# Two chunk groups into K, oT in two halves, V copied on ACT ahead of the exponentials, and a later selection in a recurrent attention kernel

## Chip, cores and metric

One core of a Trainium2 chip. The metric is device microseconds of one execution of the whole program; lower is better. Most executions of one kernel agree within 0.3%. Some versions scatter more.

PE is the matmul engine (PEld its weight loads), DVE the vector engine, ACT the scalar engine, POOL the engine that here mainly issues DMAs, SP the queue of the other DMAs.

## The reference, cut to what matters

Part A is attention with a recurrent memory: 2048 tokens in 64 segments of 32, 32 heads of 128, width 640. Eight memory rows are carried from segment to segment.

```python
mem = mem0                                   # 8 rows of 640
for s in range(64):
    h = concat([mem, x[32*s : 32*s+32]])     # 40 rows
    q, k, v = h @ Wq, h @ Wk, h @ Wv         # 640 -> 32 heads of 128
    p = softmax(mask(q @ k.T * scale))
    o = (p @ v) @ Wo                         # back to 640
    mem = o[:8]                              # the next segment needs these
    outs.append(o[8:])
```

Part B is a gated feed-forward net over all rows. It runs after the loop, and the change does not touch it.

## The kernel before

The loop is one pass per segment, fully unrolled. A helper records every operation with the keys (tiles) it reads and writes, and a solver turns keys into semaphore waits. This rule of the solver:

```python
for k in op.w:                               # keys that the operation writes
    bank = k[0] == "B"
    if k in writer:                          # it waits for the last writer of the same key
        deps[writer[k]] = deps.get(writer[k], False) or not bank
    for o in readers.get(k, ()):             # and for the readers since
        deps.setdefault(o, False)
```

The parts of a pass that the change touches, in the order in which the kernel before records them (`...` marks cuts):

```python
# K and Q projections, from the memory rows (act_r) of the pass before
project(a, ks, 1, (0, 1), BQ, spare=40)            # K, five chunks of 128
to_tok(BQ[0], 0, "act"); to_tok(BQ[1], 1, "dve")
...
project(a, ks, 0, (0, 1), (P0, P1), spare=40)      # Q
to_tok(P0, 2, "act"); to_tok(P1, 3, "dve")
...
project(a, ks, 2, (0, 1), (P2, P3), (0, 1), spare=16)       # V, chunks 0 and 1
pick_mem(T0)                                       # "selection": the memory rows of Q, 8 matmuls
copy_op("dve", Qr[:, :, q, 0:M], ..., [B(T0)], [("Qm", q)])
evac_k(KS, ("KS",), t0, nr, M, "dve")
project(a, ks, 2, (0, 1), (P2, P3), (2, 3, 4), spare=24)    # V, chunks 2 to 4
to_v(P3, Vp, 1, ("Vp",), "dve")                    # V's upper half to SBUF
scores(s)
exp_mem()                                          # ACT writes om, DVE makes Pbd from it
to_v(P2, Vp, 0, ("Vp",), "act")                    # V's lower half to SBUF
exp_x()                                            # ACT writes Px
...
filler(0); filler(1)                               # PE work of other segments, to fill waits
pv_mem(s)                                          # "memory PV": needs Pbd and Vp
...
norm_om(); filler(2); filler(3)
trans_om(...)                                      # PE transposes om, DVE copies it to oT
filler(4)
wo_pass(T1, ...)                                   # Wo: 128 small matmuls
to_act(s + 1, B(T1), bank(T1)[:, 0:160])           # memory rows, transposed, for the next K
pv_x(s, P0)                                        # PE work while DVE does to_act
```

`to_act` is one DVE transpose into TBf and one DVE cast into act_r. `spare` is room for padding: the kernel pads PE's instruction stream so that each Wo pass stands at a chosen place within a line of 256 instructions (`MARKS`). Both V copies write the same key, `("Vp",)`.

The tiles in the profile lines: `ps` is the accumulators that PE writes, `tok` the projections K and Q as copied out of them, Vp the V of this pass and Vr that of the other rows. `om` and `Px` are the exponentials of the scores (om of those against the memory rows; it later holds their result), and `Pbd` is om masked into the form that the memory PV multiplies with V.

The softmax here doesn't subtract the row's maximum and nothing guards it: scores larger than these inputs give would overflow.

## Time and profile before

The kernel before took 1122.48 us at first (median of 3) and 1121.92 us over four runs.

| of the kernel before | us or share | where it is read |
|---|---|---|
| span of the profiled run | 1118.8 | the page |
| PE busy | 95% | the page, part 1 |
| PE in the chain that ended last | 87% | the page, part 4 |
| one pass (2 to 61, mean) | 13.60 | starts of PE's groups in the timeline |

The page's first line of part 1 and the two of part 4:

```profile
PE 1063.8 (95%) x28016; PEld 505.4 (45%) x23471; DVE 593.1 (53%) x1477; ACT 353.7 (32%) x729; POOL 286.5 (26%) x575
...
PE 87%; DMA 5%; DVE 3%; SPq 3%; issue 1%; POOL 0%; ACT 0%; DVEq 0%; ACTq 0%
PE ps L419 25%; PE ps L397 24%; PE ps L636 13%; PE ps L1010 10%; PE ps L1043 3%; PE ps L564 3%; PE ps L650 3%; SPq L357 3%; DMA Wo<-in_A_Wo_dram 3%; PE ps L601 2%; DVE TBf L548 2%; PE ps L448 2%; DMA Wu<-in_B_W_up_dram 1%; DVE act_r L549 1%; PE ps L616 1%
```

PE is the bottleneck and hardly ever idle. DVE is in the chain only with TBf and act_r, the hand-over of the memory rows from Wo to the next K. ACT is not in it (0%). So the question is what happens in the few tenths of a microsecond per pass in which PE has nothing to do.

The timeline around the exponentials of pass 35. The columns are start, duration, engine, line, operation, tiles, and in brackets the idle time before it with what ended it. Scores started at S = 536.25:

```profile
536.46 0.69 DVE L461 CAST Vp<-ps 128x512 bf16<-128x512 f32 x1 [0.48 <-PE ps L397]
537.16 0.28 ACT L574 ACTIVATE om<-ps 128x128 bf16<-128x128 f32 x1 [2.67 <-PE ps L564]
537.33 0.59 ACT L459 ACTIVATE Vp<-ps 128x512 bf16<-128x512 f32 x1
537.47 0.49 DVE L577 TENSOR_TENSOR Pbd<-om,mbd 128x256 bf16<-128x256 bf16 x2 [0.32 <-ACT om L574]
537.82 0.30 PE L601 MATMUL ps<-Vr,Pbd 128*32 128x129 bf16 x8
538.07 0.30 PE L601 MATMUL ps<-Vp,Pbd 128*32 128x129 bf16 x8
```

The order om (ACT), Pbd (DVE), memory PV (PE) is a chain. PE starts the memory PV at S+1.57 here, and its filler reaches nearly up to that. ACT's V copy comes after om and holds nobody up.

From the waits of the same kernel (who waited for whom: us in total, times, longest):

```profile
PEld ps L448 <- DVE tok L461: 38.9, 61, 0.6
PEld ps L601 <- DVE Pbd L577: 33.8, 63, 0.9
ACT Vp L459 <- DVE Vp L461: 2.3, 1, 2.3
```

The last line is easily passed over: only 2.3 us. But it says that ACT's copy of V waits for DVE's. In all but one pass ACT has om to do first, so the wait does not show.

The groups of the DVE operations that the change cuts in two (count | busy, mean ns of one | idle before):

```profile
L548 DVE STREAM_TRANSPOSE TBf<-ps 128x160 f32<-128x160 f32 x64 | 22.4, 349 | 93.1 <-PE ps L636 93.0
L461 DVE COPY oT<-ps 128x256 bf16<-128x256 bf16 x63 | 18.4, 292 | 27.9 <-PE ps L616 27.9
L549 DVE CAST act_r<-TBf 128x40 bf16<-128x40 f32 x64 | 11.7, 183 | 2.2
```

And PE around selection (L448) in pass 35:

```profile
534.32 0.39 PE L397 MATMUL ps<-W,act_r 128*32 128x512 bf16 x4
534.65 0.37 PE L448 MATMUL ps<-ident,tok 128*128 128x32 bf16 x8
```

From the last group of V to selection it is 0.33 us here, where one group of four to the next takes 0.215 us. About 0.1 us is lost.

### The profile page before, as it was taken

The page shows a single profiled execution, that of the slowest core. Times are in us where ns is not written, and L with a number is a line of the kernel's source. Part 1 is how long each engine was busy: PE and PEld are TensorE (multiplying, and loading weights), DVE is VectorE, ACT ScalarE, POOL GpSimd, SP SyncE. Part 2 cuts the span into 40 slices and gives each one's busy share as a digit, 9 for nine tenths or more (in the row PEclk, how much of TensorE's full clock was granted, in tenths as well). Part 3 has the DMA queues.
Part 4 walks back from the last instruction along what each step waited for, and adds up shares of the span by engine and source line. Part 5 has one row for each costly group of instructions (what it writes and reads, how often), then busy time and mean ns, then how long its engine had stood idle before and what let it go on. Part 6 is the DMA issues. An engine that isn't in the chain of part 4 may idle for free.

```text
span 1118.8 us, 55562 instructions
## 1 busy us (share of the span) xinstructions
PE 1063.8 (95%) x28016; PEld 505.4 (45%) x23471; DVE 593.1 (53%) x1477; ACT 353.7 (32%) x729; POOL 286.5 (26%) x575
## 2 busy tenths in 40 slices
PE   5679999999999999999999999999999969999998
PEld 3344544444445454444444444444444435343443
DVE  3235555555556565666666666565656533463422
ACT  2113333333333333333433333333333312131220
POOL 1013333333333232323232414142423321000000
PEclk9879999999999999999999999999999998999999
DMA  9936454545363546465655566555544476122100
GB/s 353 381 80 109 88 110 88 108 87 108 79 111 79 111 79 107 82 122 101 117 106 114 111 115 111 100 97 93 95 89 92 91 219 173 47 77 77 24 18 24
DMA packets 290824, 122.40 MB, mean 109 GB/s; under 512 B 267008, under 2 KB 280224, under 8 KB 290592
## 3 DMA queue, kind: packets, MB, share of 16 engines
q1 hardware_dynamic: 271216, 94.95, 40.1%
q0 software_dynamic: 19184, 23.89, 9.2%
q8 instruction: 202, 3.31, 1.2%
q14 instruction: 30, 0.25, 0.1%
q10 hardware_dynamic: 192, 0.01, 0.0%
HBM read 36.79 MB, written 7.21 MB: 39 GB/s over the span
## 4 chain that ended last, share of the span: by engine, by line
PE 87%; DMA 5%; DVE 3%; SPq 3%; issue 1%; POOL 0%; ACT 0%; DVEq 0%; ACTq 0%
PE ps L419 25%; PE ps L397 24%; PE ps L636 13%; PE ps L1010 10%; PE ps L1043 3%; PE ps L564 3%; PE ps L650 3%; SPq L357 3%; DMA Wo<-in_A_Wo_dram 3%; PE ps L601 2%; DVE TBf L548 2%; PE ps L448 2%; DMA Wu<-in_B_W_up_dram 1%; DVE act_r L549 1%; PE ps L616 1%
## 5 line engine op out<-in xcount | busy, mean ns | idle before, releaser
L419 PE MATMUL ps<-W,act_r 128*32 128x512 bf16 x4277 | 398.5, 388 | 13.2 <-DMA W<-in_A_Wq_dram 3.4
L397 PE MATMUL ps<-W,act_r 128*32 128x512 bf16 x3603 | 352.8, 379 | 0.3 <-issue 0.3
L357 POOL DMA_DIRECT2D Vr<-Vp x376 | 187.5, 506 | 469.9 <-ACT Vp L459 296.1
L419 PEld LDWEIGHTS ps<-W,act_r 128*32 128x32 bf16 x4277 | 116.6, 98 | 274.6 <-issue 220.3
L459 ACT ACTIVATE tok<-ps 128x512 bf16<-128x512 f32 x191 | 110.4, 594 | 256.7 <-PE ps L397 230.1
L461 DVE CAST tok<-ps 128x512 bf16<-128x512 f32 x131 | 90.5, 691 | 148.7 <-PE ps L397 125.3
L636 PE MATMUL ps<-Wo,oT 128*32 128x160 bf16 x8320 | 160.0, 235 | 9.7 <-DMA Wo<-in_A_Wo_dram 7.4
L636 PEld LDWEIGHTS ps<-Wo,oT 128*32 128x32 bf16 x8320 | 145.3, 98 | 35.9 <-DVE oT L461 25.9
L419 PE MATMUL ps<-W,act_e 128*32 128x512 bf16 x900 | 90.9, 381 | 0.0
L397 PE MATMUL ps<-W,act_e 128*32 128x512 bf16 x900 | 90.4, 379 | 0.0
L689 DVE TENSOR_TENSOR ox<-ps,rx 128x512 bf16<-128x512 f32 x128 | 82.4, 685 | 2.2
L459 ACT ACTIVATE Qr<-QS 128x512 bf16<-128x512 bf16 (+3 forms) x107 | 70.0, 682 | 33.8 <-DMA QS<-tok 33.4
L357 POOL DMA_DIRECT2D attn_d<-wtok x64 | 46.6, 728 | 123.4 <-ACT wtok L459 123.3
L548 DVE STREAM_TRANSPOSE TBf<-ps 128x160 f32<-128x160 f32 x64 | 22.4, 349 | 93.1 <-PE ps L636 93.0
L1010 PE MATMUL ps<-xn2T,Wu 128*128 128x512 bf16 x260 | 65.7, 384 | 5.7 <-DMA Wu<-in_B_W_up_dram 5.7
L1025 DVE TENSOR_TENSOR hT<-g,ps 128x512 bf16<-128x512 bf16 (+1 forms) x56 | 38.5, 687 | 61.3 <-PE ps L1010 57.5
L1010 PE MATMUL ps<-xn2T,Wg 128*128 128x512 bf16 x246 | 62.3, 383 | 5.6 <-issue 5.3
L574 ACT ACTIVATE om<-ps 128x128 bf16<-128x128 f32 x63 | 17.5, 277 | 145.6 <-PE ps L564 142.9
L1043 PE MATMUL ps<-Wd,hT 128*128 128x320 bf16 (+1 forms) x240 | 63.3, 300 | 0.0
L1023 ACT ACTIVATE g<-ps 128x512 bf16<-128x512 f32 (+1 forms) x56 | 32.5, 592 | 95.6 <-PE ps L1010 95.6
L461 DVE CAST Vp<-ps 128x512 bf16<-128x512 f32 x64 | 44.3, 692 | 29.1 <-PE ps L397 25.1
L397 PE MATMUL ps<-Wd,hT 128*128 128x320 bf16 x208 | 56.9, 299 | 0.0
(104 smaller groups left out, 1146.4 us busy)
## 6 DMA issues: line engine op xcount, KB each, us to landing
Vr<-Vp POOLq DMA_DIRECT2D x124, 48.8 KB, 1.9
W<-in_A_Wk_dram SPq DMA_DIRECT2D x2, 2560.0 KB, 13.2
W<-in_A_Wq_dram SPq DMA_DIRECT2D x2, 2560.0 KB, 25.5
W<-in_A_Wv_dram SPq DMA_DIRECT2D x2, 2560.0 KB, 27.7
Wo<-in_A_Wo_dram SPq DMA_DIRECT2D x2, 2560.0 KB, 28.3
xt<-in_A_x_dram SPq DMA_DIRECT2D x30, 160.0 KB, 3.6
Vr<-Vp POOLq DMA_DIRECT2D x128, 32.5 KB, 1.9
attn_d<-wtok POOLq DMA_DIRECT2D x64, 40.0 KB, 2.8
```

The source lines that it names most:

```text
L357: add(eng, lambda e: e.dma_start(dst, src), r=r, w=w, dma=True)
L397: return pe.add_instruction(mybir.InstMatmult(name=nc.get_next_instruction_name(), engine=mybir.EngineType.PE, ins=[pe.lower_ap(rhs), pe.l ...
L419: ins = pe.matmul(*a, start=(c == 0), stop=(c == DC - 1), skip_group_check=True)
L459: add("act", lambda a: a.activation(dst, src, ACTF.Copy), r=r, w=w)
L461: add("dve", lambda v: v.tensor_copy(dst, src), r=r, w=w)
L548: add("dve", lambda v: v.transpose(TBf[:].rearrange("p c t -> p (c t)"), src), r=[wkey], w=[("TBf",)])
L564: i = pe.matmul(bank((P0, P1)[g % 2])[p:p + (M if a else 32), 40 * k:40 * k + 40], lh, Qr[:, h, q, :], start=True, stop=True, skip_group_c ...
L636: i = pe.matmul(bank(bk)[32 * gg:32 * gg + 32, 0:160], oT[:, hb, :], w[:, gg], start=(hb == ORDER[0]), stop=(hb == ORDER[31]), skip_group_ ...
L689: add("dve", lambda v, kh=kh: v.tensor_tensor(ox[:, :, kh, :], src[:, :, kh, 0:128], ap(rx, kh, [[2, 4], [0, 128]]), ALU.mult), r=[B(b0 + ...
L1010: ins = pe.matmul(bank(bk), w[:, c, lo:lo + 128], xn2T[par][:, c, :], start=(c == 0), stop=(c == DC - 1))
L1025: add("dve", lambda v: v.tensor_tensor(hT[par][lo:128, j, :], g1[gi][lo:128, :], bank(bu)[lo:128, :], ALU.mult), r=[B(bu), ("g1", gi)], w= ...
L1043: i = pe.matmul(*a, start=(j == 0), stop=(j == FC - 1), skip_group_check=True)
```

## The change

Its intent is to take PE's short waits away:

1. the memory rows enter act_r in two groups, chunks 0 and 1 first, so that K can start on the first group;
2. selection stands one V chunk later, so that the copy of Q that it reads is surely done;
3. oT is transposed into two banks and copied in two halves, so that the first half of Wo needs only the first copy;
4. ACT copies V before its exponentials, so that V is ready early.

```diff
     def to_act(s, wkey, src):
         b, j = s // 4, s % 4
-        add("dve", lambda v: v.transpose(TBf[:].rearrange("p c t -> p (c t)"), src), r=[wkey], w=[("TBf",)])
-        add("dve", lambda v: v.tensor_copy(act_r[b % 2][:, j, :, 0:M], TBf[:, :, 0:M]), r=[("TBf",)],
-            w=[("act", b % 2, j, "m")])
+        for n, (lo, hi) in enumerate(((0, 2), (2, DC))):
+            add("dve", lambda v, lo=lo, hi=hi: v.transpose(TBf[:, lo:hi, :].rearrange("p c t -> p (c t)"),
+                                                           src[:, 32 * lo:32 * hi]), r=[wkey], w=[("TBf", n)])
+            add("dve", lambda v, lo=lo, hi=hi: v.tensor_copy(act_r[b % 2][:, j, lo:hi, 0:M], TBf[:, lo:hi, 0:M]),
+                r=[("TBf", n)], w=[("act", b % 2, j, "mn"[n])])
 ...
     def trans_om(tile):
-        (both transposes into bank T1, one DVE copy of 256 columns, key ("oT", "m"))
+        for a, b in enumerate((T0, P3)):
+            (transpose a into bank b)
+        for a, b in enumerate((T0, P3)):
+            (DVE copy of 128 columns from bank b, key ("oT", "mn"[a]))
 ...
     # Wo, half hf
-            op = add("pe", f, r=[("oT", "m"), ("oT", "x"), ("Wo", hf)], w=[B(bk)])
+            op = add("pe", f, r=[("oT", "mn"[hf]), ("oT", "x"), ("Wo", hf)], w=[B(bk)])
 ...
-            project(a, ks, 1, (0, 1), BQ, spare=40)
+            project(a, ks, 1, (0, 1), BQ, (0, 1), spare=16)
+            ks = ks + kn
+            project(a, ks, 1, (0, 1), BQ, (2, 3, 4), spare=24)
 ...
-            project(a, ks, 2, (0, 1), (P2, P3), (0, 1), spare=16)
+            project(a, ks, 2, (0, 1), (P2, P3), (0, 1, 2), spare=24)
             (selection)
-            project(a, ks, 2, (0, 1), (P2, P3), (2, 3, 4), spare=24)
+            project(a, ks, 2, (0, 1), (P2, P3), (3, 4), spare=16)
             to_v(P3, Vp, 1, ("Vp",), "dve")
 ...
+            to_v(P2, Vp, 0, ("Vp",), "act")
             scores(s)
             exp_mem()
-            to_v(P2, Vp, 0, ("Vp",), "act")
             exp_x()
```

The lines in round brackets are cuts. The rest of the diff gives the new keys to the places that read or write them.

More of the change, by code (lines that the diff above doesn't have):

```diff
@@ L341, in build_kernel @@
         add("dve", lambda v, b=b: v.memset(bank(b), 0.0), w=[B(b)])
-    add("dve", lambda v: v.memset(oT[:], 0.0), w=[("oT", "m"), ("oT", "x")])
+    add("dve", lambda v: v.memset(oT[:], 0.0), w=[("oT", "m"), ("oT", "n"), ("oT", "x")])
     add("pool", lambda p: p.memset(ap(Vp, Dh, [[VW, 8], [1, VW - Dh]]), 1.0), w=[("Vp1",)])
@@ L345, in build_kernel @@
         add("pool", lambda p, i=i: p.memset(act_r[i][:], 0.0),
-            w=[("act", i, j, "m") for j in range(4)] + [("act", i, "x")])
+            w=[("act", i, j, h) for j in range(4) for h in "mn"] + [("act", i, "x")])
     for i in range(RING // SEG):
@@ L523, in ln1_back @@
             for e in range(2):
-                copy(act_r[1][:, e, :, :], src[:, :, 32 * e:32 * e + 32], [("act", 1, e, "m"), ("act", 1, "x")])
+                copy(act_r[1][:, e, :, :], src[:, :, 32 * e:32 * e + 32], [("act", 1, e, "m"), ("act", 1, e, "n"), ("act", 1, "x")])
             return
@@ L538, in pass_act @@
         b, j = s // 4, s % 4
-        return act_r[b % 2][:, j], [("act", b % 2, j, "m"), ("act", b % 2, "x", j), ("act", b % 2, "x")]
+        return act_r[b % 2][:, j], [("act", b % 2, j, "m"), ("act", b % 2, "x", j), ("act", b % 2, "x")], \
+            [("act", b % 2, j, "n")]
     def rider_tokens(s):
@@ L612, in trans_om, with f @@
     def trans_om(tile):
-        def f(pe):
-            for a in range(2):
+        for a, b in enumerate((T0, P3)):
+            def f(pe, a=a, b=b):
                 for c in range(0, 128, tile):
-                    i = pe.matmul(bank_bf(T1)[c:c + tile, a * 128:(a + 1) * 128], om[:, a, c:c + tile],
-                                  ident[:, :], is_transpose=True)
-            return i
-        add("pe", f, r=[("om",), ("ident",)], w=[B(T1)])
-        copy_op("dve", ap(oT, 0, [[2 * SEG, 8], [16 * SEG, 2], [SEG, 2], [1, M]]),
-                bank_bf(T1)[:, 0:256].rearrange("p (k g e q) -> p k g e q", k=8, g=2, e=2), [B(T1)], [("oT", "m")])
+                    i = pe.matmul(bank_bf(b)[c:c + tile, 0:128], om[:, a, c:c + tile], ident[:, :], is_transpose=True)
+                return i
+            add("pe", f, r=[("om",), ("ident",)], w=[B(b)])
+        for a, b in enumerate((T0, P3)):
+            copy_op("dve", ap(oT, 8 * SEG * a, [[2 * SEG, 4], [16 * SEG, 2], [SEG, 2], [1, M]]),
+                    bank_bf(b)[:, 0:128].rearrange("p (k g e q) -> p k g e q", k=4, g=2, e=2), [B(b)], [("oT", "mn"[a])])
     def head_of(n):
@@ L694, in trans_ox @@
         dma_t(oT[:].rearrange("p h t -> p (h t)").rearrange("p (k r) -> p k r", r=128),
-              ox[:].rearrange("p k g d -> p (k g d)"), [("ox", 0), ("ox", 1)], [("oT", "m"), ("oT", "x")])
+              ox[:].rearrange("p k g d -> p (k g d)"), [("ox", 0), ("ox", 1)], [("oT", "m"), ("oT", "n"), ("oT", "x")])
     def copy_oTe(s):
         o = M * (s % 4)
-        copy_op("dve", oTe[:, :, o:o + M], oT[:, :, 0:M], [("oT", "m")], [("oTe", s % 4)])
+        copy_op("dve", oTe[:, :, o:o + M], oT[:, :, 0:M], [("oT", "m"), ("oT", "n")], [("oTe", s % 4)])
     def attn_keys(i):
@@ L763, in build_kernel @@
     to_act(0, ("w0",), w0)
-    a0, k0 = pass_act(0)
-    groups = [(a0, k0)] + [(act_r[1][:, e], [("act", 1, e, "m"), ("act", 1, "x")]) for e in range(2)]
+    a0, k0, k1 = pass_act(0)
+    groups = [(a0, k0 + k1)] + [(act_r[1][:, e], [("act", 1, e, "m"), ("act", 1, e, "n"), ("act", 1, "x")]) for e in range(2)]
     gbanks = (BQ, (T0, T1), (P0, P1))
@@ L895, in build_kernel @@
         if s > 0:
-            a, ks = pass_act(s)
+            a, ks, kn = pass_act(s)
             t0, nr = rider_tokens(s)
-            project(a, ks, 1, (0, 1), BQ, spare=40)
+            project(a, ks, 1, (0, 1), BQ, (0, 1), spare=16)
+            ks = ks + kn
+            project(a, ks, 1, (0, 1), BQ, (2, 3, 4), spare=24)
             to_tok(BQ[0], 0, "act")
@@ L951, in build_kernel @@
         if s % 4 == 1 and s >= 5:
-            copy_op("dve", oTn[:, :, :], oT[:, :, 0:M], [("oT", "m")], [("oTn",)])
+            copy_op("dve", oTn[:, :, :], oT[:, :, 0:M], [("oT", "m"), ("oT", "n")], [("oTn",)])
         elif s > 0:
```

## The prediction

> **What bounds the kernel.** The page's busy table has PE at 95% of the 1118.8 us span; the chain that ended last is 87% PE. Between about 79 and 895 us run 60 alike recurrent passes of 13.6 us (timeline). The change can only win or lose in a pass's short PE stalls, read from a group's last matmul to the next group's first, starts both, less the usual step (four 512-column matmuls per 0.215 us):
> - Wo to the next K projection: DVE transpose TBf 0.35 us, then the act_r cast 0.18 us, in the chain in every pass (3% together). PE waits about 0.25 us.
> - Before selection: 0.31 instead of 0.21 us, waiting for DVE's tok copy.
> - Before Wo, in the two passes of four with 32-wide transposes: 0.345 instead of 0.206 us, behind DVE's oT copy (0.29 us).
> - Before the memory PV: only 0.03 to 0.07 us. Chain: scores start (S), ACT's om exponential at S+0.77 to 0.93, Pbd, PV at S+1.43 to 1.57.
>
> **What the change does to each.**
> 1. Two chunk groups. A DVE op here costs about 0.14 to 0.18 us plus its elements (fitted to the 160- and 40-element durations), so an estimated 0.25 + 0.155 us for the first group instead of 0.35 + 0.18: K restarts 0.14 us earlier. The second group is ready about 0.45 us after that and needed after 0.86 us: hidden. 60 passes: -8.5 us.
> 2. Selection one chunk later: the tok copy is done by then. -0.10 us each, -6 us. Its Qr copy still ends about 0.3 us before scores need it.
> 3. oT in halves: an estimated 0.22 us for a half's copy instead of 0.29, and fewer transposes ahead of it: -0.11 us in two of four passes, 0.01 to 0.03 in the others. -3.5 us.
> 4. ACT's V copy first. Both V copies write the key Vp, so the dependency solver makes ACT's copy wait for DVE's (the trace shows that semaphore on each ACT Vp copy). DVE's copy runs from S+0.21 to S+0.91; ACT's cannot start before S+0.94. Today om goes ahead of it. Behind it, om must wait: ACT goes from a 512-column copy to its next activation in 0.48 us (Vp to Px), so om starts at S+1.42 and PV at S+2.08, against a mean of S+1.53. PE has no other work there: +0.55 us in 61 passes, +33 us. The Trainium skill ("TensorE: Matmul & The Clock Gate", table of specs) calls ScalarE's queue a strict FIFO, so om cannot overtake; this trace agrees.
>
> **Sum.** 1122.5 - 8.5 - 6 - 3.5 + 33 + 1 for more semaphore waits: 1138 us, all on the critical path. Range 1129 to 1147. Faster by over 2%: 0.02; within 2%: 0.82; slower by over 2%: 0.16.
>
> **What would show it.** In the chain, Vp (DVE, ACT) and om enter with about 0.5 us per pass. PE waits about 0.6 us before the memory PV. ACT Vp starts at S+0.94, om 0.48 later. Wo's last matmul to K: 0.91 falls to 0.77 us. Step before selection 0.21 us. Pass about 13.85 us.
>
> **What would make it wrong.** ACT's copy not held by DVE's (then about 1104 us); DVE's Kr copies, now later, delaying its V copy (slower); small DVE ops costing more than fitted; instruction-fetch stalls (a hole of 0.1 to 0.15 us in scores or filler of most passes, some Wo passes of 2.5 to 3.1 us) moving.

## The result, and the profile after

The changed kernel took 1137.76 us (median of 4, 1135.76 to 1138.38) against 1121.92 us before. Ratios in this text are the mean time of one kernel's fast runs over that of the other's of the same rounds, so they are not quite the ratios of the medians that are quoted. Here the ratio is 1.0136 (95% interval 1.0117 to 1.0154): slower by 1.4%.

The same lines of the page after:

```profile
PE 1062.5 (94%) x28030; PEld 508.9 (45%) x23532; DVE 601.9 (53%) x1668; ACT 354.3 (31%) x729; POOL 287.8 (25%) x575
...
PE 81%; DVE 6%; DMA 5%; ACT 4%; SPq 3%; issue 1%; POOL 0%; DVEq 0%
PE ps L419 23%; PE ps L397 21%; PE ps L639 13%; PE ps L1015 10%; DVE Vp L461 4%; ACT Vp L459 3%; PE ps L1048 3%; PE ps L604 3%; SPq L357 3%; PE ps L677 3%; DMA Wo<-in_A_Wo_dram 3%; PE ps L653 2%; DVE Pbd L580 2%; PE ps L448 2%; DMA Wu<-in_B_W_up_dram 1%; PE ps L619 1%
```

PE's busy time did not change (1063.8 and 1062.5 us), the span grew by 17.2 us, and ACT (4%) and DVE (6%, with Vp at 4%) have entered the chain. TBf and act_r have left the list. The added time is waiting, not work.

The timeline of pass 35 again, with scores at S = 545.15:

```profile
545.37 0.69 DVE L461 CAST Vp<-ps 128x512 bf16<-128x512 f32 x1 [0.16 <-PE ps L397]
546.09 0.60 ACT L459 ACTIVATE Vp<-ps 128x512 bf16<-128x512 f32 x1 [2.70 <-DVE Vp L461]
546.59 0.27 ACT L577 ACTIVATE om<-ps 128x128 bf16<-128x128 f32 x1
546.89 0.49 DVE L580 TENSOR_TENSOR Pbd<-om,mbd 128x256 bf16<-128x256 bf16 x2 [0.83 <-ACT om L577]
547.24 0.30 PE L604 MATMUL ps<-Vr,Pbd 128*32 128x129 bf16 x8 [0.52 <-DVE Pbd L580]
547.44 0.30 PE L604 MATMUL ps<-Vp,Pbd 128*32 128x129 bf16 x8
```

ACT's copy does not start when V is there (S+0.22) but when DVE's copy has ended (S+0.94). The om exponential, now behind it on ACT, starts at S+1.43 instead of S+0.91, and PE idles 0.52 us before the memory PV, which starts at about S+2.08. The chain that ended last shows the same in order of time (start, us, what):

```profile
545.37 0.70 DVE Vp L461
546.07 0.02 issue
546.09 0.60 ACT Vp L459
546.69 0.18 ACT om L577
546.87 0.02 issue
546.89 0.30 DVE Pbd L580
547.19 0.04 issue
547.24 0.50 PE ps L604 x16
```

The waits after:

```profile
ACT Vp L459 <- DVE Vp L461: 152.6, 63, 3.0
PEld ps L448 <- DVE tok L461: 38.9, 61, 0.6
PEld ps L604 <- DVE Pbd L580: 67.8, 62, 1.5
PE ps L604 <- DVE Pbd L580: 30.6, 62, 1.4
```

The line that read "2.3, 1" before now reads "152.6, 63". (The 152.6 us are all of ACT's idle time before these copies, most of which it would have idled anyway; 63 times is the message.) The line of selection (L448) is unchanged, 38.9 us, although the copy that it names now ends long before. So that reading was wrong, as the second experiment below confirms.

The DVE groups after:

```profile
L461 DVE COPY oT<-ps 128x128 bf16<-128x128 bf16 x126 | 22.4, 220 | 24.2 <-PE ps L619 24.2
L550 DVE STREAM_TRANSPOSE TBf<-ps 128x96 f32<-128x96 f32 x64 | 17.6, 276 | 0.0
L550 DVE STREAM_TRANSPOSE TBf<-ps 128x64 f32<-128x64 f32 x64 | 16.0, 250 | 91.2 <-PE ps L639 91.2
L552 DVE CAST act_r<-TBf 128x16 bf16<-128x16 f32 x64 | 12.0, 188 | 2.2
L552 DVE CAST act_r<-TBf 128x24 bf16<-128x24 f32 x64 | 11.3, 176 | 2.2
```

The 64-column transpose takes 250 ns and the half copy of oT 220 ns. The 16-column cast takes 188 ns, no less than the 40-column cast before (183 ns).

Selection in pass 35 after:

```profile
543.66 0.39 PE L397 MATMUL ps<-W,act_r 128*32 128x512 bf16 x4
543.99 0.36 PE L448 MATMUL ps<-ident,tok 128*128 128x32 bf16 x8
```

It is still 0.33 us from the last group of V to selection.

To see all passes at once, I summed PE's stages over passes 2 to 61. A stage runs from the start of its first matmul to the start of the next stage's first, so a wait is counted in the stage before the one that waited. All sums are in us and come from the profiled run of each kernel; the experiments are explained below.

| stage | before | after | V back | V first only | two keys | ACT first |
|---|---|---|---|---|---|---|
| PV of the segment, to the next K | 44.9 | 38.9 | 39.6 | 44.7 | 40.9 | 38.2 |
| K, Q, V and selection | 415.8 | 414.7 | 420.9 | 414.3 | 420.1 | 415.6 |
| scores | 33.7 | 33.8 | 32.9 | 33.8 | 32.8 | 33.8 |
| filler 0 and 1, to the memory PV | 57.9 | 91.6 | 58.0 | 91.6 | 58.0 | 77.7 |
| memory PV | 22.0 | 19.6 | 21.9 | 19.5 | 19.6 | 19.5 |
| filler 2 and 3, transposes | 68.4 | 67.8 | 68.4 | 67.8 | 67.8 | 67.8 |
| filler 4, to Wo | 30.8 | 26.4 | 26.4 | 30.8 | 26.4 | 26.4 |
| Wo | 142.5 | 139.4 | 147.0 | 139.7 | 144.2 | 139.4 |
| 60 passes | 815.9 | 832.1 | 815.1 | 842.2 | 809.7 | 818.5 |

Before to after: the memory PV's wait costs 33.7 us. The two chunk groups give 6.0, the halves of oT 4.4, the memory PV itself 2.5, and the stage behind it 0.6. Wo gives 3.1 and the projections 1.1, which nobody had designed. The sum is +16.2.

### The profile page after: what moved, and what is told of

Same layout as the page of the kernel before. It is cut to its first block, busy times and chain, and to the rows that moved or that the text cites. A ratio compares the mean times of both kernels' runs of the same rounds, so it can differ in the third digit from the quotient of the medians.

```text
span 1136.1 us, 55767 instructions
## 1 busy us (share of the span) xinstructions
PE 1062.5 (94%) x28030; PEld 508.9 (45%) x23532; DVE 601.9 (53%) x1668; ACT 354.3 (31%) x729; POOL 287.8 (25%) x575
## 4 chain that ended last, share of the span: by engine, by line
PE 81%; DVE 6%; DMA 5%; ACT 4%; SPq 3%; issue 1%; POOL 0%; DVEq 0%
PE ps L419 23%; PE ps L397 21%; PE ps L639 13%; PE ps L1015 10%; DVE Vp L461 4%; ACT Vp L459 3%; PE ps L1048 3%; PE ps L604 3%; SPq L357 3%; PE ps L677 3%; DMA Wo<-in_A_Wo_dram 3%; PE ps L653 2%; DVE Pbd L580 2%; PE ps L448 2%; DMA Wu<-in_B_W_up_dram 1%; PE ps L619 1%
## 5 line engine op out<-in xcount | busy, mean ns | idle before, releaser
L639 PEld LDWEIGHTS ps<-Wo,oT 128*32 128x32 bf16 x8320 | 149.8, 99 | 26.5 <-DVE oT L461 16.2
L459 ACT ACTIVATE Vp<-ps 128x512 bf16<-128x512 f32 x64 | 38.3, 598 | 152.6 <-DVE Vp L461 152.6
L550 DVE STREAM_TRANSPOSE TBf<-ps 128x64 f32<-128x64 f32 (+1 forms) x128 | 33.7, 263 | 91.2 <-PE ps L639 91.2
L1030 DVE TENSOR_TENSOR hT<-g,ps 128x512 bf16<-128x512 bf16 (+1 forms) x56 | 38.6, 688 | 59.7 <-PE ps L1015 55.4
L1015 PE MATMUL ps<-xn2T,Wg 128*128 128x512 bf16 x260 | 65.7, 384 | 1.8 <-issue 1.8
L459 ACT ACTIVATE wtok<-ps 128x160 bf16<-128x160 f32 x64 | 19.5, 305 | 128.5 <-DVE TBf L550 121.9
L580 DVE TENSOR_TENSOR Pbd<-om,mbd 128x256 bf16<-128x256 bf16 x126 | 31.1, 289 | 53.5 <-ACT om L577 53.5
```

Source lines behind the costliest of these rows:

```text
L459: add("act", lambda a: a.activation(dst, src, ACTF.Copy), r=r, w=w)
L580: add("dve", lambda v, i=i: v.tensor_tensor(ap(Pbd, 256 * i, [[32, 8], [16, 2], [1, 16]]), ap(om, 0, [[16, 8], [0, 2], [1, 16]]), ap(mbd, ...
L639: i = pe.matmul(bank(bk)[32 * gg:32 * gg + 32, 0:160], oT[:, hb, :], w[:, gg], start=(hb == ORDER[0]), stop=(hb == ORDER[31]), skip_group_ ...
L1015: ins = pe.matmul(bank(bk), w[:, c, lo:lo + 128], xn2T[par][:, c, :], start=(c == 0), stop=(c == DC - 1))
L1030: add("dve", lambda v: v.tensor_tensor(hT[par][lo:128, j, :], g1[gi][lo:128, :], bank(bu)[lo:128, :], ALU.mult), r=[B(bu), ("g1", gi)], w= ...
```

## The experiments

Eleven different kernels followed, all with correct results. The first seven ask which part does what.

### V back, V first alone

The changed kernel with the V copy put back, and the kernel before with only the V copy moved:

```diff
# V back, on the changed kernel (V first alone is the reverse, on the kernel before)
-            to_v(P2, Vp, 0, ("Vp",), "act")
             scores(s)
             exp_mem()
+            to_v(P2, Vp, 0, ("Vp",), "act")
             exp_x()
```

> The changed kernel with only ACT's V copy put back behind the om exponential; the other three parts stay. Theory (the V copy's place costs 33 us and the other parts give 11 to 16): om starts at S+0.77 to 0.93 again, the memory PV at about S+1.53, time 1106 to 1112 us. Rival (the other parts give nothing, the V copy costs the whole 16 us): about 1122 us. Second rival (the new stall comes from the later selection or the halves): stays near 1138 us.

> The kernel before with only ACT's V copy moved ahead of its exponentials. Theory: ACT's copy starts at S+0.94, om at S+1.43, PV at S+2.08, about 0.55 us more in each of 61 passes, less about 2 us because V is ready earlier for the second half of the memory PV: 1152 to 1156 us. Rival (it costs only the net 16 us, the other parts are worthless): about 1138 us.

Measured: V back 1116.42 us (6 runs, 1111.78 to 1118.83), ratio to before 0.9933 (0.9908 to 0.9957). V first alone 1147.75 us (4 runs, 1146.58 to 1147.96), ratio 1.0215 (1.0192 to 1.0237).

The place of the V copy is the whole loss, and the other three parts are a gain. Both rivals fall: without the V copy's move the kernel is 0.7% faster than before, and with it alone it is slower than with all four parts. Both results lie a few us outside the expectation, on the side of "less effect". The stage table shows why. The memory PV's wait is as expected (57.9 to 91.6 us), but Wo and the projections move the other way. They are shorter where PE waits before the memory PV and longer where it does not. The section on holes below looks at that.

### Two keys

The changed kernel, order kept, but each half of Vp gets a key of its own, so ACT's copy no longer waits for DVE's. The two copies fill different columns, so this is free of races.

```diff
-            to_v(P3, Vp, 1, ("Vp",), "dve")
+            to_v(P3, Vp, 1, ("Vp", 1), "dve")
-            to_v(P2, Vp, 0, ("Vp",), "act")
+            to_v(P2, Vp, 0, ("Vp", 0), "act")
 # and every reader of Vp names both keys
```

> The changed kernel, order kept, but the two halves of Vp (different columns) get two keys, so ACT's copy no longer waits for DVE's. Theory (the wait between the two copies, not ACT's work, is the cost): ACT Vp starts at S+0.21, om at S+0.77 to 0.93, PV at S+1.43 to 1.57, time 1104 to 1112 us. Rival (ACT is simply busy 0.6 us longer ahead of om): om stays late, by about the copy's 0.48 us, and the time stays above 1125 us.

Measured: 1113.17 us (6 runs, 1108.15 to 1116.17), ratio 0.9904 (0.9879 to 0.993). Pass 35, with scores at S = 530.28:

```profile
530.49 0.69 DVE L461 CAST Vp<-ps 128x512 bf16<-128x512 f32 x1 [0.29 <-PE ps L397]
530.49 0.60 ACT L459 ACTIVATE Vp<-ps 128x512 bf16<-128x512 f32 x1 [1.97 <-PE ps L397]
531.09 0.28 ACT L577 ACTIVATE om<-ps 128x128 bf16<-128x128 f32 x1
531.74 0.30 PE L604 MATMUL ps<-Vr,Pbd 128*32 128x129 bf16 x8
```

The two copies run side by side from S+0.21, om starts at S+0.81, and the memory PV at S+1.46. ACT does the same work in the same order as in the changed kernel, so it was not ACT's work ahead of om that cost the time but the wait inside it. The time lies 1 us above the 1104 to 1112 us that were expected.

### ACT first, one key

The changed kernel with one key again, but with ACT's copy recorded before DVE's:

```diff
+            to_v(P2, Vp, 0, ("Vp",), "act")
             to_v(P3, Vp, 1, ("Vp",), "dve")
-            to_v(P2, Vp, 0, ("Vp",), "act")
             scores(s)
```

> The changed kernel, one key for both V copies, but ACT's copy stands before DVE's in the program, so that now DVE waits for ACT. Theory (whoever stands second under the one key waits for the first): ACT Vp at S+0.21, om at S+0.77 to 0.93, DVE Vp only at about S+0.85 to 1.54, and Pbd behind it on DVE: PV at about S+1.88, some 20 us more than with two keys, 1126 to 1134 us. Rival (only ACT's order matters): as with two keys, 1104 to 1112 us.

Measured: 1125.11 us (6 runs, 1123.77 to 1126.39), ratio 1.0014 (0.9993 to 1.0034). Pass 35, with S = 535.92:

```profile
536.13 0.60 ACT L459 ACTIVATE Vp<-ps 128x512 bf16<-128x512 f32 x1 [1.97 <-PE ps L397]
536.69 0.28 ACT L577 ACTIVATE om<-ps 128x128 bf16<-128x128 f32 x1
536.83 0.69 DVE L461 CAST Vp<-ps 128x512 bf16<-128x512 f32 x1 [0.99 <-ACT Vp L459]
537.77 0.30 PE L604 MATMUL ps<-Vr,Pbd 128*32 128x129 bf16 x8 [0.29 <-DVE Pbd L580]
```

Now om is early (S+0.77) and DVE's copy is late (S+0.91). Pbd stands behind it on DVE, and the memory PV starts at S+1.85. The stage before the memory PV is 77.7 us, 19.8 more than with V back or two keys. The wait belongs to whoever comes second under the shared key, and it hurts through whatever stands behind it on that engine. The time is 1 us under the expected range.

### Each other part alone, on the kernel before

Chunk groups alone: `to_act` and the two K calls of the diff above, nothing else.

> The kernel before with only the two chunk groups. Prediction said 0.14 us per pass; the trace after shows the step from Wo's end to K 0.10 us shorter: 60 passes, -6 us, 1115 to 1117 us. Rival (PE's pv work or the fetch takes it back): under 2 us.

Measured: 1119.02 us (6 runs, 1115.01 to 1124.13), ratio 0.9956 (0.993 to 0.9982). The stage from the segment's PV to K is 38.6 us in its profile, 6.3 less than before. The gain in time, 0.44% or about 5 us, agrees in size, but it is smeared by a scatter of 9 us, and the median is a miss, 2 us above the 1115 to 1117 us that were expected (the kernel before was at 1123.11 us in these rounds).

Selection alone: chunks (0, 1, 2) before it and (3, 4) after it.

> The kernel before with only the selection one V chunk later. The prediction took the 0.10 us before selection for a wait on the tok copy: then 0.21 us there and 1115 to 1117 us. New theory, from the trace after, where the step is still 0.31 us though the tok copy ended half a microsecond before: the 0.10 us is the 128-column weight load[...]; the step stays 0.31 us and the time within 1.5 us of before.

Measured: 1122.25 us (6 runs, 1119.8 to 1124.92), ratio 0.998 (0.9959 to 1.0001). I took the moment when the last tok copy ended and the start of selection's weight load, in each of the 60 passes. Before, the median distance is 0.06 us; with the later selection it is 0.49 us. PE's step into selection stays at 0.31 us (median, from the last matmul start of V). So the copy used to end just when PE could go on anyway, and taking the wait away gave nothing.

What holds PE there is therefore not the copy. The step that remains is that into a weight load of 128 columns (`128*128` in the lines) where the projections load 32. PE's step from a filler unit into the 128-column transposes in trans_om is 0.31 us as well, against 0.245 us into the 32-column ones, with the same wait on DVE. (Those two are steps from a filler projection. After the other kind of filler, Wo of earlier rows, the step into the 128-column transposes is 0.23 us.) This points to the wide weight load, but no run changed its width, so it stays argued and not shown.

Halves of oT alone: `trans_om`, the two keys, and the readers.

> The kernel before with only oT in two halves from two banks. Theory: the step before Wo falls from 0.345 to 0.22 us in the two passes of four with 32-wide transposes, hardly in the others, -4 us: 1117 to 1119 us. Rival (the second wait inside Wo costs as much): 1121 to 1123 us.

Measured: 1122.42 us (6 runs, 1119.29 to 1126.45), ratio 0.9985 (0.9963 to 1.0008): inconclusive as a time. The stage before Wo is 26.4 us, 4.4 less than before, in this kernel and in every other that has the halves. So the shorter wait is real, but the time was not the 1117 to 1119 us expected; it fell into the rival's range. The rival's reason does not hold, though: the step from Wo's first half to its second is 0.059 us in the median, in the kernel before and here. In the same profile Wo is 1.1 us longer than in the profile before, about what the stops described in the next section add in Wo (2.8 us of them before, 4.0 here), and the rest of the gain does not rise out of the scatter.

The four ratios of single parts, +2.15%, -0.44%, -0.20% and -0.15%, add up to +1.36%. The four together measured +1.36%. The middle of each small one is uncertain by 0.2 to 0.3%, so the exact agreement is chance, but nothing suggests that the parts hinder each other.

### Where part of the gain goes: holes in PE's stream

In the kernel before some Wo passes take 2.5 to 3.1 us instead of 2.33. From PE's timeline, pass 27:

```profile
430.17 1.21 PE L636 MATMUL ps<-Wo,oT 128*32 128x160 bf16 x59
432.00 0.60 PE L636 MATMUL ps<-Wo,oT 128*32 128x160 bf16 x24 [0.62 <-issue]
```

PE stops in the middle of a run of equal matmuls and waits for no semaphore ("issue"). I counted such holes in the loop: a step over 0.11 us within Wo where 0.017 is usual, or one more than 0.095 us over the usual 0.215 us within K, Q and V. Then I looked at the DMA packets of the instruction queue (q8 on the page, 202 packets of 16,384 bytes). The trace of the kernel before has 51,742 instructions of PE, weight loads and waits included: 256 for each packet, or 64 bytes an instruction.

| kernel | PE waits before the memory PV | holes | us in holes | time, lowest to highest us |
|---|---|---|---|---|
| changed | yes | 0 | 0 | 1135.8 to 1138.4 |
| V first only | yes | 0 | 0 | 1146.6 to 1148.0 |
| ACT first | yes, shorter | 3 | 0.7 | 1123.8 to 1126.4 |
| before | hardly | 11 | 3.8 | 1121.1 to 1123.9; 1118.3 to 1127.4 in the later rounds |
| V back | hardly | 26 | 10.2 | 1111.8 to 1118.8 |
| two keys | hardly | 20 | 6.2 | 1108.2 to 1116.2 |
| groups only | hardly | 15 | 5.5 | 1115.0 to 1124.1 |
| selection only | hardly | 21 | 8.1 | 1119.8 to 1124.9 |
| halves only | hardly | 11 | 4.4 | 1119.3 to 1126.5 |

The count leaves out stops between stages. In these nine kernels every hole ends 1.2 to 1.75 us after such a packet has ended. A second count, over all fourteen profiles and with PE's instructions numbered from the kernel's own offset of 64, places them: the matmul behind each of the 220 holes that it found is the second or third instruction of a block of 256. So the holes are stops at the block boundaries of PE's instruction stream.

The changed kernel and the two-key kernel have the same PE instructions at the same places. They differ only in whether PE waits about half a microsecond before the memory PV. That alone takes the holes from 20 to none, and the scatter of the times from 8 us to under 3. The size varies from run to run: that profile is of the slowest of six runs, and a later one of the same two-key kernel, of the fastest of six, has 12 holes of 3.7 us, with times 4.7 us apart. So the stall of the changed kernel also bought something: most likely it gave the instruction fetch time. Half a microsecond of waiting taken from a pass comes back only in part, because PE then runs into its own instruction supply in some passes. From changed to two keys the memory PV's wait gives 33.7 us back, Wo takes 4.8 of them again and the projections 5.4.

The Trainium skill ("Runtime: NRT & Kernel Launch", section "Instruction fetch mechanics") says that instructions come in 16 KiB blocks of 256 and that the sequencer fetches the next page while it executes the current one, so that the cost of a boundary is mostly hidden. The packets agree in size. That the cost is hidden holds in the changed kernel and in the one with V first only (no hole), and not in the other seven (up to 0.84 us for one hole in the kernel before).

Three runs tried to use this by moving the line ends of the two-key kernel and of the kernel before:

```diff
-    MARKS = (150, 98, 114, 130)
+    MARKS = (170, 118, 134, 150)    # lines end 20 instructions later
+    MARKS = (126, 74, 90, 106)      # or 24 earlier
```

> The two-key kernel with the instruction padding at the start changed so that every boundary between 256-instruction lines of PE falls 20 instructions later (the four marks plus 20). In the two-key trace the shortest line lasts 3.2 us and a 16 KB instruction fetch starts about 1.0 us after the line before begins, takes about 1.0 us, and PE crosses not before some 1.4 us after it landed: 3.4 us. Shifted by 20 the shortest line is about 3.65 us. Theory (holes in Wo and the projections are late fetches): the 6.2 us of holes fall under 3 us, 1105 to 1110 us. Rival (the holes are chance and don't depend on where lines end): as the two-key kernel, 1111 to 1115 us.

> The two-key kernel with every line boundary 24 instructions earlier (marks minus 24): the shortest line is then about 2.7 us, another about 3.1, both under the 3.4 us that a fetch needs. Theory of late fetches: a hole of 0.5 us or more in most passes that follow the passes with Wo of the early rows, 10 to 18 us more than the two-key kernel, 1122 to 1131 us. Rival (chance): 1111 to 1115 us.

> The kernel before with only the line boundaries 20 instructions later. It has 3.8 us of holes in its profile: theory of late fetches 1118 to 1121 us, so that most of the gain of the best version stays with the three parts and the two keys; rival 1121 to 1124 us.

Measured:

| run | us, median | ratio to before | holes, us |
|---|---|---|---|
| two keys, 20 later | 1114.33 (5 runs) | 0.9922 (0.9901 to 0.9943) | 15, 5.4 |
| two keys, 24 earlier | 1129.17 (6 runs) | 1.0056 (1.003 to 1.0081) | 48, 23.2 |
| before, 20 later | 1132.48 (6 runs) | 1.0085 (1.0063 to 1.0107) | 23, 9.7 |

The second run is as expected: where lines end matters, and a bad place costs 1.5% with the same work. Together with the place of the holes at the block boundaries, that rules out that they are chance.

The first and the third are misses. Ending lines later took the holes out of K, Q and V (1.8 us to 0 in the two-key kernel) but not out of Wo. On the kernel before it cost 0.85% where a small gain was expected, with 9.7 us of holes in Wo, and with stops between stages that the count above does not include, two of about 1.3 us in the filler before the memory PV and one of 1.1 us before selection. So "a line must last longer than a fetch takes" is not the whole rule. When the sequencer asks for the next block, and what it waits for until then, these profiles do not show. This stays open.

### The two-key kernel with the selection put back

> The two-key kernel with the selection put back to after two V chunks. Theory (the later selection is worth nothing, the 0.10 us before it is the 128-column weight load): within 2 us of the two-key kernel timed beside it. Rival (it is worth its 0.10 us per pass once the other stalls are gone): 4 to 7 us slower than the two-key kernel.

> The two-key kernel once more, beside the one with the selection put back: 1110 to 1116 us, ratio to before 0.988 to 0.993, as in its first rounds.

```diff
-            project(a, ks, 2, (0, 1), (P2, P3), (0, 1, 2), spare=24)
+            project(a, ks, 2, (0, 1), (P2, P3), (0, 1), spare=16)
             (selection)
-            project(a, ks, 2, (0, 1), (P2, P3), (3, 4), spare=16)
+            project(a, ks, 2, (0, 1), (P2, P3), (2, 3, 4), spare=24)
```

Measured: selection back 1107.6 us (4 runs, 1105.26 to 1108.5), ratio 0.988 (0.9859 to 0.99). The two-key kernel beside it 1110.09 us (6 runs), ratio 0.9908 (0.9891 to 0.9924). The later selection gives nothing in the combination either. With the selection put back the kernel is 2.5 us faster (medians), just outside the 2 us that were expected and in a direction that neither side had named; as a ratio it is 0.3%, and the two intervals overlap. The version with two keys, two chunk groups, halves of oT, V first and the old selection is the best: 1.2% faster than before, and 2.5% faster than the change as it was made (0.988 over 1.0136).

## Why the prediction was right

The prediction said 1138 us, and 1137.76 us were measured. The cause and the sign were right. The exact number is better than the argument behind it, because errors of the parts cancelled.

1. **V first: right in the mechanism and in the wait.** Foretold were ACT Vp at S+0.94, om at S+1.42, PV at S+2.08 and +33 us. The trace shows S+0.94, S+1.43, S+2.08 in nearly every pass, and +33.7 us in that stage. The Trainium skill's statement that ScalarE's queue is a strict FIFO ("TensorE: Matmul & The Clock Gate", table of specs) agrees: om never overtook the waiting copy, in any of 62 passes. The two-key run shows that the shared key is the cause. What the prediction left out: the memory PV itself got 2.5 us shorter, since V is there early, and the wait took the holes away (3.8 us in the kernel before, none after). As a time, the part alone cost 2.15%, about 24 us, not 33.
2. **Two chunk groups: right, too large.** "K restarts 0.14 us earlier ... -8.5 us": the trace shows 0.10 us per pass, 6.0 us. The step that failed is the estimate of "0.25 + 0.155 us for the first group". The transpose is 250 ns as foretold, but the 16-column cast takes 188 ns, no less than the 40-column one. The Trainium skill ("VectorE: DVE Perf Modes", section on the TRN2 errata) says that operations on SBUF sources pay a fixed cost per instruction, which weighs the more the smaller the operand, with a measured fixed term of about 150 cycles, which at 0.96 GHz is an estimated 156 ns; the casts of 176 to 188 ns for 16 to 40 columns lie 20 to 32 ns above that. I should not have subtracted the columns.
3. **Selection: wrong.** "-0.10 us each, -6 us": nothing came. The failed step is "waiting for DVE's tok copy". PE did start selection 0.06 us after the copy, and the waits view names the copy, but with the copy done 0.49 us before, PE's step is the same 0.31 us. Two conditions ended at nearly the same time, and I took the one that had a name. What the other is stays open; the wide weight load is the candidate.
4. **oT in halves: right.** -3.5 us foretold, -4.4 us in the stage, with 220 ns for a half copy as estimated. As a time it is inside the scatter.
5. **"About 1 us for more semaphore waits"** was not seen: PE's steps between K's two groups (0.216 us) and between Wo's halves (0.059 us) are the same before and after.
6. **"Instruction-fetch stalls moving"** was named as a danger. They did move, in favour of the changed kernel: Wo 3.1 us shorter.

The three gains together were put at 18 us and measured, with V back, at 0.67% or about 7.5 us. The loss was put at 33 us and measured alone at about 24 us. Both were overestimated by about 10 us, and the difference came out right.

## What to carry to other kernels

When two engines each write a part of one tile under one key, a dependency tracker makes the second wait for the first. As long as the second engine has other work first, that wait is invisible, and moving the copy forward turns it into a stall of everything queued behind it. Before you reorder, list the semaphores of the instruction that you move and ask when each is released; give disjoint parts their own keys.

A releaser that the profile names is the last of possibly several conditions: a step that stays at its value when the named one is done earlier was held by another. And in a kernel whose engine is nearly always busy, count the stops with no releaser too, because the instruction supply can take back a part of what a removed wait gives.

## What the Trainium skill lacked or had wrong

- "Runtime: NRT & Kernel Launch", section "Instruction fetch mechanics", calls the cost of a 16 KiB boundary mostly hidden. Here PE stopped for up to 0.84 us in the kernel before, 3.8 us in its loop, and 23.2 us with lines that end 24 instructions earlier. How long before a boundary the fetch must have landed is on no page; in nine kernels the holes ended 1.2 to 1.75 us after a packet of that queue had ended (up to 2.4 us in the five later profiles).
- No page says that a wait put in front of a dense stretch can take such holes away: 20 holes with two keys (12 in a second profile), none in the changed kernel with the same PE instructions.
- "TensorE: Matmul & The Clock Gate", Part 3, has in its list of what overlaps that weight loads overlap running matmuls only when their row groups differ. The projections here load all 128 rows of one column group (128*32) and still step at 0.215 us per four matmuls with the loads under way. (The same part also says that a load into the background weight buffer is pulled ahead; its list does not.) The step into a 128*128 load is 0.31 us. The page has a formula for the length of one load by its columns, but no figure for that step.
- "VectorE: DVE Perf Modes", section on the TRN2 errata, takes its fixed term from operands of 512 and 2048 elements. For small ones: a cast of 16, 24 or 40 columns from SBUF took 188, 176 and 183 ns, a transpose of 64, 96 or 160 columns from PSUM 250, 276 and 349 ns.
